# Scattered rows of a fused long convolution and mixture of experts: smaller staging units, another spread of the row DMAs, fewer cleared pages, no flush

## The chip, the cores and the metric

The kernel runs on one core of a Trainium2 chip. The time is device microseconds of one execution, first to last instruction and what the runtime lays around it; the median of several runs counts. Five engines work beside each other, each through its own list of instructions, strictly in order: TensorE (PE, matrix products; PEld is its weight load), VectorE (DVE), ScalarE (ACT), GpSimd (POOL) and SyncE (SP, which only starts DMAs). An instruction that waits holds everything behind it in its own list, and nothing else.

## What is computed

Cut to its core, the reference is a causal convolution over 10048 positions by way of Fourier transforms, for 4 batch entries of 128 channels, gated by its input, and then a mixture of experts: each of the 40192 rows goes to one of 16 experts, a two-layer network 128 to 1024 to 128.

```python
y = irfft(rfft(x * v, 2 * S) * rfft(h_filt, 2 * S)[None], 2 * S)[:, :S]
x = (x * y).reshape(4 * 10048, 128)
for g in range(4):                 # group by argmax of x @ w_group
    for e in range(4):             # expert by argmax of x @ w_expert[g]
        h = np.maximum(x[mine] @ w1[g, e], 0.0)
        out[mine] = g_w * e_w * (h @ w2[g, e])
```

## The kernel before

**Stages.** Batch entries are called batches 0 to 3 here. After the filter's own transform the function `conv` runs a loop over b. Each pass has two stages. The first is the forward transform of batch b (43 parts of three channels, `dft_blocks`) together with the inverse transform of batch b - 1 (22 steps j, `turned` and `inverse_blocks`, which ends in the product with x, L692). The second, 40 steps of two frequencies each, multiplies by the filter's spectrum: `middle` (two products on DVE, L605 and L608, then a sum and a difference on POOL, L606 and L609, which write a tile y) and, four steps later, `back` (the matmul that reads y, L617). The last pass, b = 4, has only the inverse transform of batch 3. In the trace these stages are called here forward/inverse 1, 2, 3 (inverse of batches 0, 1, 2), middle 0, 1, 2, 3, the last inverse, the last choice of experts, and the experts.

**Routing.** When a batch's rows are there, `chosen` writes them to HBM (`xyd`) and computes expert and weight of each row; `ranked` then counts rows per expert and computes for each row its address `adr` in a paged buffer `prow` in HBM. A page holds 256 rows of one expert. Both are generators, of which one step at a time is taken between the steps of the stages; so the routing of batch b runs in the middle stage b + 1 and at the head of the next stage.

**Rows into pages.** A batch's rows stand in 79 blocks of 128. Each block is one indirect DMA, started by POOL (`put`, L343), which writes its 128 rows to the addresses in `adr`. The rows come from HBM through a staging tile `stg`: `stage` starts the load on SP (L335) and adds the row's number and weight by a small copy on POOL (L336). Load and copy write a buffer that earlier puts read, and so wait until these have landed. Before the puts of a batch come eight indirect DMAs that empty the open ends of its last pages (`clear`, L357). All of these stand in a list `self.scatters`; each call of `scatter(n)` issues up to n of them, so the calls' arguments in `conv` spread them over the stages. Pages that hold no row of the first assignment are emptied once, by plain DMAs from POOL in middle 1 (`clear_rest`, L326).

**POOL's other work.** In the forward/inverse stages 2 and 3 POOL also computes a difference for each part (`eo`, L437) that the forward transform needs; in the last inverse every other product L692; among the experts, the low half of one weight matrix per page (`wl`, L1224) and the indirect DMAs that write the output (L1280).

**Experts.** `work` runs 164 pages, one after the other, in a software pipeline. `fetch` issues the scatters that are left, early enough for the pages that need them. `rest` handles pages beyond the 164 if there are any.

**Buffers of the last inverse.** `xo` (the gate's input, loaded on SP, L660) and `yt` (L689, L690) take turns in one ring of four buffers.

A scheduler may move instructions that no fixed order holds; most of those named here are held in program order on their engine.

Of the kernel before, what the change touches and what calls it, by code (L numbers as in the profile page):

```python
# [12 lines left out]
F32 = mybir.dt.float32  # L13
# [30 lines left out]
RW = 130  # L44
ZR = 4
LAGS = 3
STG = 2
EVERY = 2
LATER = 48
CHOSEN = -(-NB // 4) + 2  # L50
# [83 lines left out]
class Kernel:  # L134
# [59 lines left out]
    def conv(self, ctx, right):  # L194
        tc, nc, d = self.tc, self.nc, self.d
        cp = ctx.enter_context(tc.tile_pool(name="cconst", bufs=1))
        zp = ctx.enter_context(tc.tile_pool(name="z", bufs=1))
        self.psA = ctx.enter_context(tc.tile_pool(name="psA", bufs=3, space=PSUM, reuse_waits="tile"))
        self.psT = ctx.enter_context(tc.tile_pool(name="psT", bufs=3, space=PSUM, reuse_waits="tile"))
        self.psO = ctx.enter_context(tc.tile_pool(name="psO", bufs=2, space=PSUM, reuse_waits="tile"))  # L200
        self.psr = lambda shape, name: self.psO.tile(shape, F32, tag="po", name=name)
        self.fa = cp.tile([NR, 2, 2 * NB], F32, name="fa")

        self.z = zp.tile([128, KM + 16, 2, 128], F32, name="z")
        nc.vector.memset(self.z[:, NB:], 0.0)
        ahead = ExitStack()
        made, folded = [], []
        with ExitStack() as c2:
            self.filter(c2, ahead, made, folded)
        bp = ctx.enter_context(tc.tile_pool(name="back", bufs=1))  # L210
        self.fi = bp.tile([128, 2, 5, NB], F32, name="fi")
        nc.sync.dma_start(self.fi.rearrange("p h a t -> p (h a t)"), d["c_fi"])


        inner = ExitStack()
        xyp = inner.enter_context(tc.tile_pool(name="xy", bufs=1, reuse_waits="tile"))
        self.sp = inner.enter_context(tc.tile_pool(name="stream", bufs=2, reuse_waits="tile"))
        routing, self.scatters = iter(()), []

        self.anchor, self.loose = None, []  # L220
        for b in range(self.nbat + 1):
            last = b == self.nbat
            if last:
                ahead.close()
                inner.close()
                self.sp = ctx.enter_context(tc.tile_pool(name="stream", bufs=2, reuse_waits="tile"))
                weights = self.first_weights(right)
                xy = self.z.rearrange("p k s d -> p (k s) d")[:, :NB]
            elif b > 0:
                xy = xyp.tile([128, NB, D], F32, tag="xy", name=f"xy{b - 1}")  # L230
            parts = groups(D, GD) if not last else []
            if b == 1:
                self.router_consts()
            self.run_ahead(b, 0, made, folded)
            for j, (d0, n) in enumerate(groups(120, GI) + [(120, 4), (124, 4)]):
                if b > 0 and j % 2 == 0:
                    tts = self.turned(d0, min(2 * GI, D - d0))
                for i in range(2 * j, min(2 * j + 2, len(parts))):
                    self.run_ahead(b, i, made, folded)
                    self.scatter(1 + (i % 4 == 0))  # L240
                    self.dft_blocks(*folded[i])
                    if b > 0 and i % 2 == 0:
                        self.inverse_blocks(b - 1, xy, d0, n, tts)
                if last:
                    self.inverse_blocks(b - 1, xy, d0, n, tts)
                    next(weights, None)
                    if j == 1:
                        for p in self.all[:XG]:
                            p.load()
                for _ in range(3 if last else 1):  # L250
                    next(routing, None)
                if last:
                    self.scatter(1 + j % 2)
            made, folded = [], []
            if b > 0:
                oh = self.rp.tile([128, NE, NB], F32, tag="oh", name="oh")
                en = self.entries.tile([128, NB, 2], F32, tag="en", name="en")
                routing = chain(self.chosen(b - 1, xy, oh, en), self.ranked(b - 1, oh, en))
                if last:
                    for _ in range(CHOSEN):  # L260
                        next(routing)
            if not last:
                back = []
                for i, (k0, n) in enumerate(groups(NB, 2)):
                    back.append(self.middle(b, k0, n))
                    if len(back) > LAG:
                        self.back(*back.pop(0))
                    if b == 1 and i % 4 == 1:
                        self.clear_rest(i // 4)
                    self.scatter(NB if b == self.nbat - 1 and i == 37 else i < 37)  # L270
                    if i % 4 != 3 if i < 30 else i % 2:
                        next(routing, None)
                for args in back:
                    self.back(*args)
        return routing
# [44 lines left out]
    def clear_rest(self, i):  # L320

        q0 = self.nbat * SEQ // TP
        qs = range(q0, self.pages.n)[i::10]
        for q in qs:
            dst = self.d["prow"][q * TP : q * TP + TP].rearrange("(p z) c -> p z c", z=ZR)
            self.tc.keep_in_program_order(self.nc.gpsimd.dma_start(dst, self.empty[: TP // ZR]))  # L326

    def stage(self, k):

        while self.staged <= min(k, len(self.units) - 1):  # L330
            u = self.units[self.staged]
            n = u.n
            u.rows = self.entries.tile([128, 4, RW], F32, tag="stg", name="stg", bufs=STG)
            src = self.d["xyd"][u.b * 128 * NB : (u.b + 1) * 128 * NB].rearrange("(p t) c -> p t c", p=128)
            self.nc.sync.dma_start(u.rows[:, :n, 0:128], src[:, u.t0 : u.t0 + n])  # L335
            self.beyond(self.nc.gpsimd.tensor_copy(u.rows[:, :n, 128:130], u.en[:, u.t0 : u.t0 + n]))  # L336
            self.staged += 1

    def put(self, u, t):

        self.stage(u.k + STG - 1)
        n = self.pages.n * TP
        ins = self.nc.gpsimd.indirect_dma_start(  # L343
            self.d["prow"],
# [308 lines left out]
    def inverse_blocks(self, b, xy, d0, n, tts):  # L653
# [30 lines left out]
                )  # L684
        oo = sp.tile([64, GI, NB], F32, tag="oo", name="oo")
        nc.scalar.copy(oo[:, :n], po[64:128, :n])
        pool, tag, bufs = (self.ap, "y", NY) if b < self.nbat - 1 else (sp, "spec", NSPEC)
        yt = pool.tile([128, GI, NB], F32, tag=tag, name="yt", bufs=bufs)
        nc.vector.tensor_tensor(yt[0:64, :n], po[0:64, :n], oo[:, :n], ALU.add)  # L689
        nc.vector.tensor_tensor(yt[64:128, :n], po[0:64, :n], oo[:, :n], ALU.subtract)  # L690
# [108 lines left out]
    def ranked(self, b, oh, en):  # L799
# [122 lines left out]
        v.memset(pos[64:128, NB - 1 : NB], BIGID)  # L922
        adr = self.entries.tile([128, NB], I32, tag="adr", name="adr")
        v.tensor_copy(adr, pos)
        for t0, n in groups(NB, 4):
            u = Unit(b, len(self.units), t0, n, adr, en)
            self.units.append(u)
            self.scatters += [(b, lambda u=u, t=t: self.put(u, t), self.tick + LAGS, u) for t in range(t0, t0 + n)]
# [96 lines left out]
    def rest(self, count, q):  # L1025

        with self.tc.If(count > q):
            self.work(self.all[q : q + 4])
            if q + 4 < self.pages.n:
                self.rest(count, q + 4)  # L1030

# [351 lines left out]
```

## Time and profile before

| what | us |
|---|---|
| median of three runs | 2227.9 |
| lowest and highest of them | 2226.0, 2235.4 |
| the profiled execution, whole | 2243.6 |
| its span, first to last instruction | 2241.8 |
| PE busy in it (89%) | 2006.3 |
| DVE busy (77%) | 1719.4 |
| POOL busy (63%) | 1402.3 |
| ACT busy (61%) | 1364.4 |

The profile is of one execution. Shares over the whole span mix stages with different limits: the experts (from about 1166 us on) are a dense stretch of matmuls, while in the stages of the convolution different engines set the pace. So the tables of the prediction are by stage. In a row of groups stand the line, engine, operation, tiles (written from read), shape and count, then busy time and mean duration in ns of one, then the idle time of the engine just before them with what ended it. In a row of waits stand who waited for whom, the total in us, how often, and the longest. In a row of stretches stand each engine's busy time with its number of instructions, the clock that PE was granted, the share of the DMA engines and GB/s. Timeline rows begin with start and duration in us.

### The profile page before, as it was taken

The page shows a single profiled execution, that of the slowest core. Times are in us where ns is not written, and L with a number is a line of the kernel's source. Part 1 is how long each engine was busy: PE and PEld are TensorE (multiplying, and loading weights), DVE is VectorE, ACT ScalarE, POOL GpSimd, SP SyncE. Part 2 cuts the span into 40 slices and gives each one's busy share as a digit, 9 for nine tenths or more (in the row PEclk, how much of TensorE's full clock was granted, in tenths as well). Part 3 has the DMA queues.
Part 4 walks back from the last instruction along what each step waited for, and adds up shares of the span by engine and source line. Part 5 has one row for each costly group of instructions (what it writes and reads, how often), then busy time and mean ns, then how long its engine had stood idle before and what let it go on. Part 6 is the DMA issues. An engine that isn't in the chain of part 4 may idle for free. (4 is left out here: it accounts for less than half of the span.)

```text
span 2241.8 us, 54150 instructions
## 1 busy us (share of the span) xinstructions
PE 2006.3 (89%) x18062; PEld 1824.2 (81%) x18062; DVE 1719.4 (77%) x3647; ACT 1364.4 (61%) x3005; POOL 1402.3 (63%) x1521
## 2 busy tenths in 40 slices
PE   8989999987888788885879999999999999999997
PEld 8867787766766577664659999999999999999996
DVE  5687776896567776668459989899899778888885
ACT  6642454433443244332458888888878778888885
POOL 2167402886778866785525667688878785555554
PEclk9999999988899788998989999999999999999998
DMA  4798756965677655774654444546555554444442
GB/s 126 250 247 283 223 149 199 360 195 165 172 243 265 190 142 169 243 267 149 206 176 136 128 143 143 149 145 184 151 151 159 153 146 133 129 128 125 125 125 61
DMA packets 260641, 394.26 MB, mean 176 GB/s; under 512 B 33319, under 2 KB 133266, under 8 KB 260352
## 3 DMA queue, kind: packets, MB, share of 16 engines
q1 hardware_dynamic: 225024, 318.01, 46.9%
q0 software_dynamic: 25824, 57.16, 7.3%
q10 hardware_dynamic: 9504, 15.54, 2.7%
q8 instruction: 146, 2.39, 0.5%
q14 instruction: 143, 1.17, 0.2%
HBM read 303.24 MB, written 88.37 MB: 175 GB/s over the span
## 5 line engine op out<-in xcount | busy, mean ns | idle before, releaser
L1244 DVE SCALAR_TENSOR_TENSOR hl<-ph,hh 128x512 fp32r<-128x512 f32 x656 | 445.9, 685 | 117.2 <-ACT hh L1243 91.8
L1243 ACT ACTIVATE hh<-ph 128x512 fp32r<-128x512 f32 x656 | 393.3, 605 | 130.5 <-PE ph L1237 68.7
L1280 POOL DMA_INDIRECT out<-os,to x328 | 347.4, 1059 | 93.7 <-issue 80.8
L1254 PE MATMUL py<-hh,wh 128*128 128x256 f32 x1312 | 398.7, 304 | 0.0
L343 POOL DMA_INDIRECT prow<-stg,adr x316 | 344.7, 1091 | 82.1 <-issue 47.7
L1256 PE MATMUL py<-hh,wl 128*128 128x256 f32 x1312 | 373.9, 285 | 12.8 <-POOL wl L1224 12.3
L1235 PE MATMUL ph<-xh,wh 128*128 128x256 f32 x1312 | 373.3, 284 | 4.3 <-ACT wh L1217 2.5
L1237 PE MATMUL ph<-xh,wl 128*128 128x256 f32 x1312 | 373.1, 284 | 0.6 <-DVE wl L1224 0.6
L1236 PE MATMUL ph<-xl,wh 128*128 128x256 f32 x1312 | 372.6, 284 | 0.0
L1255 PE MATMUL py<-hl,wh 128*128 128x256 f32 x1312 | 371.6, 283 | 0.0
L1224 POOL TENSOR_TENSOR wl<-ws,wh 128x512 fp32r<-128x512 f32 x162 | 219.5, 1355 | 220.5 <-ACT wh L1217 216.9
L1256 PEld LDWEIGHTS py<-hh,wl 128*128 128x128 f32 x1312 | 251.6, 192 | 16.3 <-POOL wl L1224 16.3
L1235 PEld LDWEIGHTS ph<-xh,wh 128*128 128x128 f32 x1312 | 252.9, 193 | 5.0 <-ACT wh L1217 2.7
L1237 PEld LDWEIGHTS ph<-xh,wl 128*128 128x128 f32 x1312 | 253.0, 193 | 1.2 <-DVE wl L1224 1.2
L1236 PEld LDWEIGHTS ph<-xl,wh 128*128 128x128 f32 x1312 | 253.0, 193 | 0.1
L624 ACT COPY z<-pbp 128x512 f32<-128x512 f32 (+1 forms) x160 | 92.6, 581 | 263.3 <-PE pbp L617 225.9
L1255 PEld LDWEIGHTS py<-hl,wh 128*128 128x128 f32 x1312 | 252.8, 193 | 0.0
L1254 PEld LDWEIGHTS py<-hh,wh 128*128 128x128 f32 x1312 | 252.0, 192 | 0.0
L1224 DVE TENSOR_TENSOR wl<-mw,wh 128x512 fp32r<-128x512 f32 x328 | 233.5, 712 | 0.0
L447 PE MATMUL psb<-z,bt 128*128 128x256 f32 x790 | 203.6, 389 | 33.1 <-DMA bt<-c_b 15.4
L606 POOL TENSOR_TENSOR y<-t 128x256 f32<-128x256 f32 (+1 forms) x160 | 119.3, 746 | 167.1 <-DVE t L605 161.4
L1217 ACT CAST wh<-ws 128x512 fp32r<-128x512 f32 x328 | 206.6, 630 | 10.1 <-PE ph L1237 8.4
(232 smaller groups left out, 4488.7 us busy)
## 6 DMA issues: line engine op xcount, KB each, us to landing
ws<-m_w SPq DMA_DIRECT2D x328, 256.0 KB
ht<-hspec SPq DMA_DIRECT2D x156, 256.0 KB
xv<-xv_in SPq DMA_DIRECT2D x131, 288.0 KB
bt<-c_b SPq DMA_DIRECT2D x95, 256.0 KB
xg<-prow SPq DMA_DIRECT2D x164, 130.0 KB
bp<-c_bp SPq DMA_DIRECT2D x76, 256.0 KB
stg<-xyd SPq DMA_DIRECT2D x76, 256.0 KB
xyd<-xy SPq DMA_DIRECT2D x57, 256.0 KB
```

Source lines behind the costliest of these rows:

```text
L343: ins = self.nc.gpsimd.indirect_dma_start(self.d["prow"], bass.IndirectOffsetOnAxis(ap=u.adr[:, t : t + 1], axis=0), u.rows[:, t - u.t0], ...
L1217: k.fix(k.nc.scalar.copy(hi, self.matrix(i, half, self.ea)))
L1224: ins = v.tensor_tensor(lo, self.matrix(i, half, self.ed), self.wh[i][half].bitcast(F32), ALU.subtract)
L1235: k.fix(nc.tensor.matmul(ph[:, j], wh, self.xh, start=True, stop=False))
L1236: k.fix(nc.tensor.matmul(ph[:, j], wh, self.xl, start=False, stop=False))
L1237: k.fix(nc.tensor.matmul(ph[:, j], wl, self.xh, start=False, stop=True))
L1243: k.fix(nc.scalar.activation(hh, ph, AF.Relu))
L1244: k.fix(nc.vector.scalar_tensor_tensor(hl, ph, 0.0, hh.bitcast(F32), ALU.max, ALU.subtract))
L1254: k.fix(nc.tensor.matmul(self.py, wh, self.hh[c], start=(c == 0), stop=False))
L1255: k.fix(nc.tensor.matmul(self.py, wh, self.hl[c], start=False, stop=False))
L1256: k.fix(nc.tensor.matmul(self.py, wl, self.hh[c], start=False, stop=(c == NC - 1)))
L1280: ins = k.nc.gpsimd.indirect_dma_start(k.d["out"], bass.IndirectOffsetOnAxis(ap=self.to[:, h : h + 1], axis=0), o[:, h], None, bounds_chec ...
```

## The change

Six things change. A staging unit has two blocks instead of four, and there are four buffers instead of two, which is the same memory. The refill is started at the first put of a unit for the unit two ahead, into the buffer of the unit two back, instead of one ahead into the buffer of the unit just finished. The row DMAs are spread in another way: in the forward/inverse stage one per part, and from part 12 on two at every odd part (before: one, and two at every fourth); in the middle stage three in four steps (before: one at each of the first 37 steps). At step 37 of the last middle stage nothing is flushed any more; what is left goes out in the last inverse, and the first page loads move from its step 1 to its step 8, behind the puts of batches 0 and 1. `clear_rest` empties 7 pages instead of 47, and pages beyond 164 are each guarded by an own condition. In the last inverse `yt` has a ring of two buffers of its own, and `xo` keeps the ring of four.

```diff
-STG = 2
+UB, STG = 2, 4
@@ conv, forward/inverse stage
-                    self.scatter(1 + (i % 4 == 0))
+                    self.scatter(1 + (i >= 12 and i % 2))
...
-                    if j == 1:
+                    if j == 8:
+                        self.scatter(sum(1 for s in self.scatters if s[0] < self.nbat - 2))
                         for p in self.all[:XG]:
                             p.load()
@@ conv, middle stage
-                    self.scatter(NB if b == self.nbat - 1 and i == 37 else i < 37)
+                    self.scatter(i % 4 != 3)
@@ clear_rest
-        qs = range(q0, self.pages.n)[i::10]
+        qs = range(q0, self.pages.usual)[i::10]
@@ stage
-            u.rows = self.entries.tile([128, 4, RW], F32, tag="stg", name="stg", bufs=STG)
+            u.rows = self.entries.tile([128, UB, RW], F32, tag="stg", name="stg", bufs=STG)
@@ put
-        self.stage(u.k + STG - 1)
+
+        self.stage(u.k + STG // 2)
@@ inverse_blocks
-        pool, tag, bufs = (self.ap, "y", NY) if b < self.nbat - 1 else (sp, "spec", NSPEC)
+        pool, tag, bufs = (self.ap, "y", NY) if b < self.nbat - 1 else (sp, "yt", 2)
@@ ranked
-        for t0, n in groups(NB, 4):
+        for t0, n in groups(NB, UB):
@@ rest
-            self.work(self.all[q : q + 4])
+            self.work(self.all[q : q + 1])
+            for p in self.all[q + 1 : q + 4]:
+                with self.tc.If(count > p.q):
+                    self.work([p])
```

The lines of the kernel after stand two lower from `put` on (L345 is the put, L337 the copy, L439 the difference, L608 and L611 the sums, L694 the last product, L359 the clears).

**Forward/inverse 2, list of POOL, a stretch of its second half.** L437 is the difference of a part; the number behind `stg` names the buffer's filling. Before:

```order
L437 TENSOR_TENSOR eo_6834<-xv_6778 96x3x64
L336 COPY stg_6837<-en_4438 128x4x2
L343 DMA prow<-stg_6680,adr_6068 52224x130 x2
L437 TENSOR_TENSOR eo_6882<-xv_6831 96x3x64
L343 DMA prow<-stg_6680,adr_6068 52224x130
L437 TENSOR_TENSOR eo_6899<-xv_6879 96x3x64
L343 DMA prow<-stg_6680,adr_6068 52224x130
L437 TENSOR_TENSOR eo_6941<-xv_6896 96x3x64
L336 COPY stg_6944<-en_4438 128x4x2
```

The same stretch of the list after the change:

```order
L439 TENSOR_TENSOR eo_7227<-xv_7201 96x3x64
L345 DMA prow<-stg_7103,adr_6028 52224x130
L439 TENSOR_TENSOR eo_7269<-xv_7224 96x3x64
L337 COPY stg_7272<-en_4438 128x2x2
L345 DMA prow<-stg_7162,adr_6028 52224x130 x2
L439 TENSOR_TENSOR eo_7328<-xv_7266 96x3x64
L337 COPY stg_7331<-en_4438 128x2x2
L345 DMA prow<-stg_7210,adr_6028 52224x130
L439 TENSOR_TENSOR eo_7373<-xv_7325 96x3x64
L345 DMA prow<-stg_7210,adr_6028 52224x130
L337 COPY stg_7379<-en_4438 128x2x2
```

Before, the copy into a new filling (6944) stands right behind the last put of the unit whose buffer it takes over, and four puts come between copies. After, a copy (7331) takes over a buffer whose puts stand a whole unit further back (the two puts of 7162 lie between), a copy comes after every two puts, and there are three puts to two differences.

**End of middle 3 and head of the last inverse, list of POOL.** L606 and L609 make the y tiles of the last steps, L357 the clears, L692 products of the last inverse. Before:

```order
L609 TENSOR_TENSOR y_12105<-t1_12109 128x2x128
L343 DMA prow<-stg_11996,adr_9413 52224x130 x3
L606 TENSOR_TENSOR y_12160<-t0_12161 128x2x128
L606 TENSOR_TENSOR y_12175<-t0_12176 128x128
L609 TENSOR_TENSOR y_12175<-t1_12179 128x128
L357 DMA prow<-empty_81,fidx_11955 13056x520 x8
L609 TENSOR_TENSOR y_12160<-t1_12164 128x2x128
L692 TENSOR_TENSOR z_103<-yt_12325,xo_12304 128x6x79
```

After:

```order
L345 DMA prow<-stg_12048,adr_9433 52224x130
L608 TENSOR_TENSOR y_12222<-t0_12223 128x128
L611 TENSOR_TENSOR y_12222<-t1_12226 128x128
L345 DMA prow<-stg_12123,adr_9433 52224x130
L694 TENSOR_TENSOR z_103<-yt_12375,xo_12354 128x6x79
L337 COPY stg_12430<-en_10819 128x2x2
L345 DMA prow<-stg_12123,adr_9433 52224x130
L337 COPY stg_12436<-en_10819 128x2x2
L345 DMA prow<-stg_12187,adr_9433 52224x130
L359 DMA prow<-empty_81,fidx_12026 13056x520
L694 TENSOR_TENSOR z_103<-yt_12528,xo_12507 128x6x79
L359 DMA prow<-empty_81,fidx_12026 13056x520 x3
```

Eight clears stood ahead of the last difference that makes a y; now they stand between the products of the last inverse, and the y tiles have one put at a time between them.

**Last inverse, list of SP.** L660 (L662 after) loads `xo`, L997 (L999) the experts' weights, L335 (L336) fills a staging buffer. Before:

```order
L335 DMA stg_12874<-xyd 128x4x128
L660 DMA xo_12919<-x_out 128x474
L997 DMA mw1_12217<-m_w1 128x2x512
L660 DMA xo_12948<-x_out 128x474
L997 DMA mw1_12217<-m_w1 128x2x512
L335 DMA stg_12977<-xyd 128x4x128
L660 DMA xo_13019<-x_out 128x474
```

After:

```order
L336 DMA stg_12904<-xyd 128x2x128
L662 DMA xo_12910<-x_out 128x474
L999 DMA mw1_12264<-m_w1 128x2x512
L336 DMA stg_12939<-xyd 128x2x128
L662 DMA xo_12981<-x_out 128x474
L999 DMA mw1_12264<-m_w1 128x2x512
L662 DMA xo_13010<-x_out 128x474
L999 DMA mw1_12264<-m_w1 128x2x512
L336 DMA stg_13036<-xyd 128x2x128
```

Before, a refill stands ahead of every second load of `xo`; after, refills of half the size stand ahead of two in three, and each waits for puts issued a unit earlier.

## The prediction

> **What bounds the kernel now.** I read the stretches by stage first, since shares of the whole span mix stages with different limits.
>
> ```profile
> core 0: us, PE busy (x) PEld busy (x) DVE busy (x) ACT busy (x) POOL busy (x), PEclk, DMA share, GB/s
> 252.00:372.00 120.00, 109.46 (x1556) 96.34 (x1558) 90.88 (x185) 60.39 (x108) 2.06 (x4) 0.94 0.55 151
> 372.00:471.00 99.00, 91.16 (x585) 71.23 (x581) 83.09 (x198) 38.80 (x93) 78.55 (x121) 0.98 0.95 322
> 471.00:628.00 157.00, 125.70 (x1594) 106.49 (x1594) 110.30 (x194) 62.45 (x111) 111.86 (x132) 0.86 0.58 168
> 628.00:747.00 119.00, 96.08 (x563) 72.68 (x563) 82.79 (x193) 39.10 (x93) 95.42 (x123) 0.95 0.79 257
> 747.00:903.00 156.00, 127.78 (x1594) 107.93 (x1594) 110.79 (x222) 61.34 (x111) 104.90 (x124) 0.84 0.56 160
> 903.00:1045.00 142.00, 102.26 (x581) 75.96 (x577) 101.04 (x271) 40.51 (x95) 111.41 (x139) 0.89 0.66 228
> 1045.00:1131.00 86.00, 73.07 (x1061) 61.11 (x1062) 45.50 (x68) 37.45 (x65) 36.61 (x39) 0.96 0.58 190
> 1166.00:1450.00 284.00, 275.85 (x2258) 273.87 (x2259) 254.42 (x593) 234.90 (x529) 181.44 (x162) 0.98 0.47 140
> 1450.00:1870.00 420.00, 400.31 (x3296) 394.55 (x3295) 363.67 (x698) 339.83 (x761) 338.55 (x319) 1.00 0.52 155
> 1870.00:2242.00 372.00, 355.55 (x2985) 354.91 (x2983) 287.06 (x622) 306.41 (x686) 207.18 (x177) 0.98 0.39 117
> ```
>
> The rows are forward/inverse 1, middle 1, forward/inverse 2, middle 2, forward/inverse 3, middle 3, the last inverse, and three stretches of the experts. The stages without puts are much shorter: forward/inverse 120 us against 157 and 156, middle 99 against 119 and 142. PE is busy 91 of 99 us in middle 1 but only 126 of 157 in forward/inverse 2. Among the experts PE is busy over 95%, so little can be gained there. Next the waits, first over the whole span and then of the last inverse, to see what puts have to do with it.
>
> ```profile
> POOL stg L336 <- DMA prow<-stg,adr: 70.7, 39, 3.8
> SPq L335 <- DMA prow<-stg,adr: 290.3, 78, 9.2
> ...
> SPq L335 <- DMA prow<-stg,adr: 31.6, 7, 9.2
> DVE z L692 <- DMA xo<-x_out: 18.3, 7, 4.3
> PE po L670 <- DVE yt L690: 9.9, 4, 4.1
> ```
>
> POOL stands 70.7 us in the small copy, until the last put of the buffer's old unit has landed, and SP 290 us in the refill, with everything queued behind it. Whether that counts is told by POOL's groups in stretches where puts run: forward/inverse 2 (530 to 620 us), forward/inverse 3 (815 to 895) and middle 2 (640 to 730).
>
> ```profile
> L343 POOL DMA_INDIRECT prow<-stg,adr x35 | 38.6, 1102 | 9.1 <-issue 5.1 <-POOL stg L336 3.2 <-DVE yt L690 0.6
> L437 POOL TENSOR_TENSOR eo<-xv 96x192 f32<-96x192 f32 x26 | 21.1, 812 | 0.5
> L336 POOL COPY stg<-en 128x8 f32<-128x8 f32 x8 | 2.8, 349 | 19.0 <-DMA prow<-stg,adr 19.0
> ...
> L343 POOL DMA_INDIRECT prow<-stg,adr x30 | 34.7, 1156 | 8.4 <-issue 4.0 <-POOL stg L336 2.3 <-DVE xv L423 1.5
> L437 POOL TENSOR_TENSOR eo<-xv 96x192 f32<-96x192 f32 x23 | 14.9, 650 | 0.4
> L336 POOL COPY stg<-en 128x8 f32<-128x8 f32 x8 | 2.1, 266 | 20.1 <-DMA prow<-stg,adr 15.7 <-issue 4.4
> ...
> L343 POOL DMA_INDIRECT prow<-stg,adr x29 | 29.1, 1003 | 8.4 <-issue 4.6 <-POOL stg L336 3.8
> L609 POOL TENSOR_TENSOR y<-t 128x256 f32<-128x256 f32 x29 | 22.6, 780 | 0.0
> L606 POOL TENSOR_TENSOR y<-t 128x256 f32<-128x256 f32 x29 | 21.9, 755 | 2.7 <-DVE t L605 2.2
> L336 POOL COPY stg<-en 128x8 f32<-128x8 f32 x6 | 1.4, 237 | 6.0 <-DMA prow<-stg,adr 6.0
> ```
>
> In the first stretch the busy times and the idle times add up to 91 of 90 us: **POOL never waits for anybody but its own puts**. So POOL sets the pace there, and PE gets its differences (L437) or sums (L606, L609) only as fast as POOL comes to them. The stall of 19 us in 90 is on the path; so is every put, and every copy.
>
> **The change part by part.** Durations are of this execution, 2243.6 us long (span 2241.8); the three plain runs have a median of 2227.9, 15.7 less, so I take the difference from the profile off the median.
>
> *Forward/inverse 2.* A put costs (38.6 + 9.1 - 3.2) / 35 = 1.27 us with its gap, a difference 0.81, a copy with the gap behind it (2.8 + 3.2) / 8 = 0.75. Before, 26 parts took 90 us, 6.92 per two parts. After, from part 12 on, two parts carry three puts, two differences and 1.5 copies without stall: 3.81 + 1.62 + 1.13 = 6.56. Over 15.5 pairs that is 5.6 us less: **-6**. The stall goes, but most of it is paid back in more puts (54 puts and clears in the stage against 49) and in twice the copies. The new refill could stall too; two puts and two differences, about 4 us, now lie between the old unit's last put and the copy, and the longest stall so far was 3.8. I take it as gone.
>
> *Forward/inverse 3.* The same sum from its own rows: put 1.36, difference 0.65, copy 0.55; 80 us for 23 parts, 6.96 per pair; after 4.08 + 1.30 + 0.83 = 6.21. Over 15.5 pairs **-12**. Both stages cannot go below the pace of forward/inverse 1, 120 us for 21.5 pairs, 5.58.
>
> *Middle 2 and 3.* 29 steps took 90 us, 3.10 each. After, a step has both sums (22.6 + 21.9 + 2.7) / 29 = 1.63, 0.75 puts of 1.16, and 0.375 copies of 0.9: 0.87 + 0.33 + 1.63 = 2.83. Over 38 steps -10; SP no longer holds the loads of the spectrum behind a refill, for which I add 2: **-12 each**. The floor is middle 1, 99 us for 40 steps, 2.48.
>
> *The flush.* POOL's list and PE at the end of middle 3, and that stretch:
>
> ```profile
> 1029.58 0.45 POOL L609 TENSOR_TENSOR y<-t 128x128 f32<-128x128 f32 x1
> 1030.20 1.05 POOL L357 DMA_INDIRECT prow<-empty,fidx  x1 [0.17 <-issue]
> ...
> 1040.14 1.12 POOL L357 DMA_INDIRECT prow<-empty,fidx  x1 [0.30 <-issue]
> 1041.28 0.74 POOL L609 TENSOR_TENSOR y<-t 128x256 f32<-128x256 f32 x1
> 1042.08 1.22 PE L617 MATMUL pbp<-y,bp 128*128 128x256 f32 x2 [15.17 <-POOL y L609]
> ...
> 1029.00:1042.00 13.00, 0.00 (x0) 0.00 (x0) 12.93 (x50) 0.00 (x0) 10.69 (x12) 0.50 0.52 191
> ```
>
> Eight clears hold one sum back by 11 us, and PE stands 15.2. But DVE was busy 12.93 of those 13 us, with `ranked`. That work does not vanish: it now falls beside the products of the last inverse, on the same DVE, which is busy 45.5 of 86 us there and has room, though not at its head. Between 0 and 15, I take half: **-8**. The eight clears go to POOL's list in the last inverse, which then issues four puts fewer, 25 against 29, and POOL is busy only 37 of 86 us there.
>
> *The last inverse.* DVE waits 18.3 us for `xo`, whose load stands behind a refill on SP (31.6 us in seven waits) and behind a ring that it shares with `yt`. Both go. What reached PE is nearer to its own 9.9 us of waiting for `yt`: between 0 and 18, **-7**.
>
> *Clearing.*
>
> ```profile
> L326 POOL DMA_DIRECT2D prow<-empty x47 | 25.0, 538 | 0.0
> ```
>
> Forty issues of 0.54 us leave POOL in middle 1 and 5.2 MB leave a stage whose DMA share is 0.95. But PE was busy 91 of its 99 us, so between 0 and 8: **-2**.
>
> *The experts.*
>
> ```profile
> PE py L1256 <- POOL wl L1224: 12.3, 13, 2.5
> ```
>
> Here POOL gets more: 67 refills against 31, 36 copies of 0.75, and seven puts of batch 2 that were done earlier before; 27 + 9 us, less a few us of stall. In the first two stretches POOL is busy 181 of 284 and 339 of 420 us, so most of it hides in 184 free us; if that cover were gone it would cost 36, and at best the 12.3 us vanish. I take **+3**. The conditions for pages beyond 164 are not entered either way: 0, as in the row of the last stretch, which has only the pages' matmuls.
>
> Sum: -6 - 12 - 12 - 12 - 8 - 7 - 2 + 3 = **-56**. 2243.6 becomes 2188 for such an execution, and the median 2227.9 becomes **2172**.
>
> **Rivals.** *Half of it.* POOL's time is read from rows in which it shares the stage with a busy DVE; with the stalls gone DVE runs denser, puts and copies stretch, and other waits (DVE for its input, PE for ACT) take over part of it. For it speaks that puts took 1.10 and 1.16 us in the forward/inverse stages against 1.00 in middle 2. Half of 56 gives 2200.
>
> *The floor.* Once POOL is out of the way, stages fall to the pace of those without puts: 15.5 x (6.92 - 5.58 and 6.96 - 5.58) = 42 and 38 x 2 x (3.10 - 2.48) = 47, with flush, inverse and clearing at 15, 10 and 2: -116, 2112. Against it: three puts, two differences and the copies cannot be issued in 5.58 us by the rows above.
>
> *Another wait in its place.* The puts land no earlier than before, and a refill of half the size starts a transfer twice as often; if the refill itself arrives late, the stall only moves from the copy to the put. Then the spread and the extra puts eat the rest: about 2222. Against it: a filling is asked for four puts, some 8 us, ahead of its use, as before.
>
> *Slower: the copies.* Each of the 80 added copies stands in the list of the engine that sets the pace.
>
> ```profile
> L336 POOL COPY stg<-en x80: 182/193/1052, 509.8 to 1835.8; 128x8 f32<-128x8 f32 x76, 128x6 f32<-128x6 f32 x4
> ```
>
> The longest took 1.05 us. At that price, 0.70 above mine, the 93 copies that the stages of the convolution have after the change (against 49) add 65 us, and a quarter of the 67 among the experts 12: +21 in all, 2249. It decides from a copy of 0.75 + 56 / 93 = 1.35 us on. Against it stands the median of 193 ns. The Trainium skill, "SBUF — State Buffer", section "Who interferes with whom", speaks for it: a GpSimd instruction that reads SBUF is kept out for the whole length of a VectorE instruction with two SBUF inputs, and such instructions are what DVE runs in the forward/inverse stages. The row of before agrees in that copies there mean 349 and 266 ns against 237 in middle 2, but shows a full instruction's wait only in its maximum.
>
> **How the numbers follow.** About 0.5%, 11 us, is what a measurement of this kernel can tell from no change. The forecast, 2172, gets 0.60: POOL's sums close on their windows, and the removed stall and flush are read directly. Half gets 0.17, the floor 0.10, another wait 0.08, slower copies 0.05. Faster by over 0.5% are the first three, 0.87; within 0.5% 0.08; slower 0.05. The forecast's own bounds (flush 0 to 15, last inverse 0 to 18, clearing 0 to 8, experts -12 to +36) reach some 35 us to either side; half's 2200 lies inside, the floor is taken in only in part: 2132 to 2212.
>
> **What would show it.** Right: POOL's wait for landed puts falls from 70.7 us to below 10 and SP's 290 to a fraction; forward/inverse 2 and 3 last about 151 and 144 us, middle 2 about 107; middle 3 has no gap of PE near 15 us, and middle 3 with the last inverse together take some 200 instead of 228; DVE no longer waits for `xo`; the experts last as long as before within a few us. Wrong: copies near 1 us, a wait of puts for the refill in place of the old one, a last inverse that grows by what middle 3 lost because `ranked` holds up `yt`, or experts in which PE's 12.3 us of waiting for `wl` have doubled.

## The result, and the profile after

Before: median 2228.0 us of 4 runs (2226.0 to 2235.4). After: **2166.8** (2165.1 to 2174.2). The ratio is 0.9726, 95% interval 0.9694 to 0.9758, so the change saves 61 us. The forecast was 2172, with a range of 2132 to 2212. The profiled execution after the change took 2168.2 us, close to its median, while the one of before (2243.6) lay 15.6 above its own. So a second execution of before was profiled (span 2220.7), and the stages below are held against that one.

The stretches of the changed kernel, from one stage's first matmul to the next's, in the columns of the prediction's first table: middle 1, forward/inverse 2, middle 2, forward/inverse 3, middle 3, last inverse, experts.

```profile
core 0: us, PE busy (x) PEld busy (x) DVE busy (x) ACT busy (x) POOL busy (x), PEclk, DMA share, GB/s
370.60:461.60 91.00, 86.51 (x564) 69.30 (x560) 77.50 (x199) 38.00 (x91) 60.36 (x85) 1.00 0.91 298
461.60:606.60 145.00, 122.23 (x1595) 104.84 (x1595) 110.41 (x191) 62.80 (x112) 121.75 (x149) 0.88 0.62 178
606.60:723.40 116.80, 97.42 (x577) 74.72 (x575) 82.25 (x194) 39.96 (x95) 90.42 (x124) 0.95 0.84 263
723.40:872.20 148.80, 122.16 (x1582) 103.99 (x1582) 110.22 (x222) 61.18 (x109) 120.36 (x141) 0.85 0.59 169
872.20:991.10 118.90, 100.36 (x581) 76.94 (x577) 87.45 (x212) 41.19 (x96) 92.97 (x129) 0.93 0.74 242
991.10:1080.50 89.40, 71.66 (x1069) 60.45 (x1069) 66.04 (x132) 38.99 (x65) 49.75 (x54) 0.96 0.67 217
1103.50:2166.40 1062.90, 1028.35 (x8537) 1021.84 (x8537) 917.99 (x1917) 874.45 (x1973) 755.16 (x696) 0.99 0.47 140
```

Middle 1 takes 91.0 us, with PE at full clock (1.00); forward/inverse 2 and 3 are still 25 to 29 us longer than forward/inverse 1 (120.2). Middle 2, forecast at 107, stands at 116.8. The waits over the whole span, which answer to the rows of POOL's copy, SP's refill and the loads of `xo` before:

```profile
SPq L336 <- DMA prow<-stg,adr: 426.1, 141, 11.6
...
DVE z L694 <- DMA xo<-x_out: 15.9, 4, 4.7
...
PE py L1261 <- POOL wl L1229: 11.7, 18, 1.3
...
POOL z L694 <- DMA xo<-x_out: 4.1, 1, 4.1
...
POOL stg L337 <- DMA prow<-stg,adr: 2.1, 5, 0.8
```

POOL's wait for landed puts went from 70.7 to 2.1 us, as forecast. SP's wait in the refill did not fall to a fraction of 290: **it rose to 426**. Per wait it is a little shorter (426.1 / 141 = 3.0 against 290.3 / 78 = 3.7 us), but there are nearly twice as many (the second profile of before has 327.1 us in 92 waits). DVE still waits 15.9 us for `xo`, which was to vanish.

### The profile page after: what moved, and what is told of

Its sections match the earlier page's. It is cut to its first block, busy times and chain, and to the rows that moved or that the text cites. A ratio compares the mean times of both kernels' runs of the same rounds, so it can differ in the third digit from the quotient of the medians.

```text
span 2166.4 us, 54337 instructions
## 1 busy us (share of the span) xinstructions
PE 1986.7 (92%) x18062; PEld 1816.9 (84%) x18062; DVE 1728.6 (80%) x3647; ACT 1360.1 (63%) x3005; POOL 1421.5 (66%) x1561
## 4 chain that ended last, share of the span: by engine, by line
PE 59%; DVE 11%; DMA 7%; POOL 7%; issue 4%; ACT 1%; SPq 0%; ACTq 0%; POOLq 0%; DVEq 0%
PE py L1261 7%; PE py L1259 7%; PE py L1260 7%; PE ph L1242 7%; PE ph L1240 7%; PE ph L1241 7%; PE psb L449 3%; PE pbp L619 3%; DMA ht<-hspec 2%; PE psa L378 2%; DMA xv<-xv_in 2%; POOL prow L345 2%; PE ptm L1273 2%; PE px L1197 2%; POOL out L1285 1%
## 5 line engine op out<-in xcount | busy, mean ns | idle before, releaser
L1285 POOL DMA_INDIRECT out<-os,to x328 | 357.2, 1089 | 92.8 <-issue 74.6
L345 POOL DMA_INDIRECT prow<-stg,adr x316 | 345.7, 1094 | 70.4 <-issue 35.3
L1261 PE MATMUL py<-hh,wl 128*128 128x256 f32 x1312 | 373.8, 285 | 11.7 <-POOL wl L1229 11.7
L1261 PEld LDWEIGHTS py<-hh,wl 128*128 128x128 f32 x1312 | 251.1, 191 | 15.9 <-POOL wl L1229 15.6
L608 POOL TENSOR_TENSOR y<-t 128x256 f32<-128x256 f32 (+1 forms) x160 | 117.2, 732 | 202.8 <-DVE t L607 195.6
L1229 DVE TENSOR_TENSOR wl<-mw,wh 128x512 fp32r<-128x512 f32 x328 | 245.3, 748 | 0.0
L449 PE MATMUL psb<-z,bt 128*128 128x256 f32 x790 | 203.9, 389 | 34.5 <-DMA bt<-c_b 15.1
L1222 ACT CAST wh<-mw 128x512 fp32r x328 | 206.7, 631 | 0.0
```

The lines of the kernel that those rows point to most:

```text
L345: ins = self.nc.gpsimd.indirect_dma_start(self.d["prow"], bass.IndirectOffsetOnAxis(ap=u.adr[:, t : t + 1], axis=0), u.rows[:, t - u.t0], ...
L449: nc.tensor.matmul(ps[:, i], bt[:, i], self.z[:, k0 + i], start=True, stop=True,)
L1229: ins = v.tensor_tensor(lo, self.matrix(i, half, self.ed), self.wh[i][half].bitcast(F32), ALU.subtract)
L1261: k.fix(nc.tensor.matmul(self.py, wl, self.hh[c], start=False, stop=(c == NC - 1)))
L1285: ins = k.nc.gpsimd.indirect_dma_start(k.d["out"], bass.IndirectOffsetOnAxis(ap=self.to[:, h : h + 1], axis=0), o[:, h], None, bounds_chec ...
```

## The experiments

Two theories stood after this result. *The sum holds*: POOL's stall and the flush were the price, and each part is worth what its term says. *SP has taken over*: a refill that waits on SP holds the loads of the spectrum (`ht`, `bt`) and of `xo`, so the middles lost their gain to a new wait. Stage durations in us, each from PE's first matmul of a stage to that of the next, read off the timeline of each run's profile; the median is that of the run's timed executions. Each row is one execution: the two profiles of before differ by up to 4.0 us in a stage and by 10.0 among the experts, so a single difference below that is weak evidence by itself.

| kernel | fwd/inv 2 | middle 2 | fwd/inv 3 | middle 3 | last inv. | experts | span | median |
|---|---|---|---|---|---|---|---|---|
| before, second profile | 153.6 | 119.3 | 153.3 | 140.0 | 97.4 | 1068.1 | 2220.7 | 2222.5 (one) |
| units alone | 151.0 | 118.0 | 151.2 | 135.9 | 80.9 | 1057.9 | 2186.3 | 2189.6 |
| spread alone | 160.7 | 121.5 | 153.8 | 139.4 | 95.5 | 1070.0 | 2229.7 | 2234.4 |
| no flush alone | 154.4 | 119.3 | 155.7 | 124.1 | 95.9 | 1077.4 | 2214.0 | 2218.4 |
| ring alone | 153.2 | 123.3 | 153.0 | 139.7 | 96.9 | 1068.8 | 2224.5 | 2225.0 |
| clears alone | 154.2 | 120.9 | 153.3 | 144.0 | 94.5 | 1067.6 | 2217.9 | 2219.4 |
| after | 145.0 | 116.8 | 148.8 | 118.9 | 89.3 | 1062.9 | 2166.4 | 2166.8 |
| after, large units | 161.9 | 116.9 | 157.3 | 123.0 | 96.5 | 1071.7 | 2210.1 | 2211.9 |
| after, old spread | 151.0 | 114.7 | 148.5 | 117.1 | 84.8 | 1063.4 | 2165.1 | 2174.5 |
| after, with flush | 144.5 | 114.6 | 148.8 | 137.4 | 82.3 | 1056.3 | 2168.9 | 2171.8 |
| after, one ahead | 148.2 | 105.3 | 147.9 | 107.9 | 80.3 | 1059.9 | 2133.4 | **2138.9** |
| after, refill on POOL | 154.7 | 111.4 | 151.3 | 120.6 | 86.8 | 1089.8 | 2198.7 | 2204.5 |
| one ahead, two in inverse | 145.2 | 104.4 | 150.8 | 107.9 | 93.4 | 1053.6 | 2138.3 | 2140.9 |

Middle 1 lasts 91.0 in every kernel without the 40 clears and 95.7 to 97.8 in the others.

**The kernel before once more** (no edit).

> The kernel before once more, for a second profiled execution. The experts of the first one lasted 1078.1 us, those of the changed kernel 1062.9, though nothing in the change should shorten them. If the 15 us are that one execution (it was 2243.6 against a median of 2227.9), this profile's experts last 1060 to 1066 and its other stages stay within 1 to 2 us: 120.9, 98.0, 157.2, 118.7, 155.8, 142.4, 93.4 for forward/inverse 1, middle 1, forward/inverse 2, middle 2, forward/inverse 3, middle 3, last inverse. If the change does shorten the experts, they last 1075 to 1081 again, and a whole execution is near 2243.

The experts lasted 1068.1 us: 10 of the 15 us were that one execution, 5 are left for the change. In the three kernels below with the same puts among the experts and large units (spread, ring and clears alone) they last 1067.6 to 1070.0, so it is the first execution that stands apart; PE waited 13.7 us there for ACT's copy `ys`, against 5.3 in the second. The other stages moved by 4 us at most, more than the 1 to 2 expected.

**Units alone** (the lines that take the size from `UB`, in `stage` and `ranked`, are left out here).

```diff
-STG = 2
+UB, STG = 2, 4
-        self.stage(u.k + STG - 1)
+        self.stage(u.k + STG // 2)
```

> The kernel before with the staging units alone: two blocks, four buffers, two units ahead. If POOL's stall is on the path and sets the pace of the forward/inverse stages, removing 19 us of 90 and 20 us of 80 there and paying one more copy per four puts (0.75 us each) leaves -13 in each of the two stretches, some -18 in each whole stage, about 0 in the middles (6 us of stall against 7 us of copies): -35 to -45 in all, near 2188, and this part is most of the gain. If the change gains by its other spread of the puts and the units only make it possible, this gives -10 or less (2218 or more). SP: if its wait in the refill grows because a refill now waits for puts that were issued shortly before, its waits are above 380 us here too, against 290 before.

Ratio 0.9840 (0.9807 to 0.9873): the total fits the first theory, the places do not. Forward/inverse 2 and 3 gave 2.6 and 2.1 us, not 18 each; the last inverse gave 16.5 and the experts 10.2. POOL's waits in forward/inverse 2, before (second profile) and with small units:

```profile
POOL stg L336 <- DMA prow<-stg,adr: 18.6, 9, 3.9
...
POOL eo L437 <- PE psa L376: 3.0, 2, 2.2
```

```profile
POOL eo L437 <- PE psa L376: 18.8, 10, 3.0
```

The stall of 18.6 us left, and a wait of 18.8 us for PE took its place: with the old spread POOL was the pace only as long as it stalled. Where the gain was instead, the last inverse shows. Its stretch before (second profile):

```profile
1032.20:1129.50 97.30, 76.97 (x1068) 64.10 (x1069) 46.79 (x72) 38.37 (x65) 44.26 (x46) 0.89 0.55 177
```

and with small units:

```profile
1023.90:1104.80 80.90, 69.88 (x1068) 59.40 (x1068) 46.63 (x72) 38.31 (x65) 46.97 (x56) 0.99 0.66 214
```

The waits in these two stretches, before first:

```profile
DVE z L692 <- DMA xo<-x_out: 25.9, 8, 5.5
...
POOL z L692 <- DMA xo<-x_out: 18.8, 6, 4.9
...
PE po L670 <- DVE yt L690: 12.7, 5, 4.1
```

```profile
DVE z L692 <- DMA xo<-x_out: 21.7, 8, 4.5
...
POOL z L692 <- DMA xo<-x_out: 7.3, 5, 2.6
...
PE po L670 <- DVE yt L690: 4.9, 4, 1.6
```

PE waits 7.8 us less for `yt`, and its 1068 matmuls take 7.1 us less at a granted clock of 0.99 instead of 0.89. SP's wait was 419 us here, above the 380 named: the longer wait comes with the units.

**Spread alone** (both `scatter` arguments of the change, the flush kept).

> The kernel before with the other spread of the puts alone, the flush and the large units kept. Each middle has 0.25 puts of 1.16 us less per step, -11 in middle 2 and in middle 3; each forward/inverse stage has about five puts more, each with its share of stall some 1.8 us, +9. Additive parts: -4 in all, same (2224). If the middles are paced by POOL, middle 2 shortens to 108; if another engine or SP's held loads pace it, it stays above 114, and the whole is slower, 2235.

Ratio 1.0047 (1.0029 to 1.0065). Middle 2 did not get shorter (121.5): it still held 35 puts, as before, because forward/inverse 2 passed only the same 44 in its 160.7 us and left the added six over, ahead of the middle's first sum in POOL's list. With the stall in that list more puts to a part only pile up.

**No flush alone.**

```diff
-                    if j == 1:
+                    if j == 8:
+                        self.scatter(sum(1 for s in self.scatters if s[0] < self.nbat - 2))
-                    self.scatter(NB if b == self.nbat - 1 and i == 37 else i < 37)
+                    self.scatter(i < 37)
```

> The kernel before without the flush at step 37 of the last middle stage, and with the first page loads at step 8. The prediction's term says -8 (0 to -15): PE's gap of 15.2 us goes, and the routing's work on DVE falls beside the last inverse, which grows by some 7. If PE's gap was the whole price, middle 3 with the last inverse shortens by 15. If DVE's work is what had to be done anyway, they shorten by 0 to 2.

Middle 3 and the last inverse lost 17.4 us together: PE's gap was the whole price there, and `ranked` on DVE did not hold the inverse up. But the kernel gained only 5 (ratio 0.9978, 0.9960 to 0.9996): the experts were 9.3 longer, with 133 puts among them instead of 127, and PE's wait for `wl` there went from 13.0 to 19.4.

**Ring alone** (`yt` in two buffers of its own).

> The kernel before with the own ring for yt alone. The prediction put -7 on the last inverse for this and for the smaller refills together, and the units alone already shortened that stage from 97.4 to 80.9 us. If the shared ring is what makes SP late with xo, the ring alone gives -5 or more there (below 92). If it is the refill that SP stands in, the ring alone gives 0 to -2, DVE's and POOL's waits for xo stay at some 40 us together, and the whole is the same (2222 to 2227).

Ratio 1.0001 (0.9982 to 1.0021), last inverse 96.9 against 97.4: the shared ring had no price that shows.

**Clears alone** (7 pages instead of 47, own conditions beyond page 164).

> The kernel before with 7 cleared pages instead of 47 and an own condition for each page beyond 164. The prediction said -2 in middle 1 (0 to -8). In the changed kernel middle 1 lasts 91.0 us against 97.1 and 98.0. If the missing clears are the whole reason, middle 1 lasts 90 to 92 here and every other stage as before: -6 to -7, near 2218. If the conditions beyond 164 cost time at the end, the whole gains less than middle 1 does.

Ratio 0.9968 (0.9951 to 0.9985), 7 us, and middle 1 went from 97.1 to 91.0. The conditions cost nothing. The end of the program even got shorter: from PE's last matmul to the end of the span 14.2 us in the second profile of before and 11.7 here, and no more than 11.9 in any kernel that has this edit. What fills the time behind the last output there the profiles do not show.

**The change with the old spread.**

```diff
-                    self.scatter(1 + (i >= 12 and i % 2))
+                    self.scatter(1 + (i % 4 == 0))
-                    self.scatter(i % 4 != 3)
+                    self.scatter(i < 37)
```

> The changed kernel with the old spread: one put per part and two at every fourth, one at each of the first 37 steps of a middle. Alone, on the kernel before, the new spread cost time (ratio 1.0047, some +10 us; forward/inverse 2 grew by 7 us). If the parts add up, taking it out of the changed kernel gains 10 us: 2157. If the spread needs the small units (without a stall behind every unit the doubled puts no longer pile up), taking it out costs: forward/inverse 2 back to 151, as with the units alone, forward/inverse 3 to 151, the middles 1 to 3 longer: 2174 to 2180.

The ratio to before is 0.9784 (0.9753 to 0.9816), against 0.9726 for the whole change; the intervals just overlap, and its four runs lie between 2166.9 and 2179.0. Forward/inverse 2 went back to 151.0 as the second theory of the expectation says, but the middles and the last inverse got shorter, by 1.8 to 4.5 us; the profiled execution (2166.9) is also the lowest of the four. With small units the new spread is worth between nothing and 8 us; alone it cost 10.

**The change with large units.**

```diff
-UB, STG = 2, 4
+UB, STG = 4, 2
-        self.stage(u.k + STG // 2)
+        self.stage(u.k + STG - 1)
```

> The changed kernel with four blocks to a unit, two buffers, refilled one unit ahead, as before; spread, ring, clears and the missing flush stay. If the units alone are worth what they gave on the kernel before (ratio 0.984, 35 us), this is 2202. If spread and units lean on each other, the other parts without the units are worth no more than -10 to -15 together: 2210 to 2215, with POOL's stall in the copy back at 65 to 75 us and PE's wait for wl among the experts above that of the changed kernel (11.7 us).

Ratio 0.9947 (0.9930 to 0.9964): without the units the rest is worth 12 us, with them the change is worth 61. Units alone gave 35, so they and the rest lean on each other by some 14 us, above all in forward/inverse 2 (units alone 151.0, the rest alone 161.9, both 145.0): three puts to two parts are paid only where no stall of 77.9 us stands in POOL's list.

**The refill one unit ahead.**

```diff
-        self.stage(u.k + STG // 2)
+        self.stage(u.k + 1)
```

> The changed kernel with one edit: the refill started at the first put of a unit is for the next unit, into the buffer of three units back, instead of two ahead into the buffer of two units back. Middle 2 lasts 116.8 us in the changed kernel, where 107 was predicted; SP waits 426 us in the refill and DVE 26.7 for the spectrum, PE 15.1 for its table. Theory, SP holds the middles: the wait of the refill for the unit before last holds the loads behind it; with a buffer whose puts lie a unit further back SP's wait falls below 150 us, the two waits of 42 us together fall below 20, and middle 2 and 3 shorten by 6 to 10 us each: 2147 to 2155. Rival, the middles are paced by DVE and POOL: SP's wait falls as much, the middles stay within 2 us of 116.8 and 118.9, the whole is 2160 to 2170. Second rival, the refill comes too late: puts wait for the load of their own rows, 1 us or more at each of some 40 units, and the whole is 2180 to 2210.

**2138.9 us, ratio 0.9619 (0.9596 to 0.9642), faster than both kernels.** The middles fell to 105.3 and 107.9, the last inverse to 80.3. The waits of middle 2: before (second profile), after, and one ahead.

```profile
SPq L335 <- DMA prow<-stg,adr: 52.3, 13, 6.1
...
DVE t L605 <- DMA ht<-hspec: 8.4, 5, 4.1
POOL stg L336 <- DMA prow<-stg,adr: 8.4, 6, 2.5
...
PE psb L447 <- DMA bt<-c_b: 7.0, 4, 3.2
...
POOL y L606 <- DVE t L605: 6.2, 3, 2.8
```

```profile
SPq L336 <- DMA prow<-stg,adr: 52.4, 16, 6.8
...
DVE t L607 <- DMA ht<-hspec: 16.6, 7, 5.1
POOL y L608 <- DVE t L607: 16.4, 15, 2.6
...
PE psb L449 <- DMA bt<-c_b: 5.7, 3, 4.8
```

```profile
SPq L336 <- DMA prow<-stg,adr: 32.7, 12, 6.1
...
DVE t L607 <- DMA ht<-hspec: 9.0, 4, 3.9
POOL y L608 <- DVE t L607: 8.5, 4, 3.0
...
PE psb L449 <- DMA bt<-c_b: 0.5, 1, 0.5
```

Read down the chain: SP stands in the refill, the spectrum comes late, DVE waits for it, POOL waits for DVE. In the change POOL's 8.4 us of stall had turned into 16.4 us of waiting for DVE. One unit ahead, the refill takes over the buffer of three units back, whose puts lie two further back in POOL's list. SP's wait over the whole span fell only to 376, not below 150, since it stayed as it was in the forward/inverse stages and among the experts (179 us), where it holds nothing that is late; in the two middles and the last inverse it fell by 60 of 152 us. Puts waited 0.9 us in all for their own rows. The waits for the spectrum and for PE's table `bt` fell from 41.8 us together to 28.5, not below 20: in middle 2 both fell, but in middle 3, which gained 11 us as well, the table's fell from 7.5 to 0.3 and the spectrum's rose from 8.9 to 13.2. There PE idled 4.9 us less and its matmuls took 5.7 less, at a granted clock of 0.98 instead of 0.93. That SP's refill wait holds the middles is so shown by the edit; through which of the held loads, only for middle 2.

**The refill issued by POOL.**

```diff
-            self.nc.sync.dma_start(u.rows[:, :n, 0:128], src[:, u.t0 : u.t0 + n])
+            self.beyond(self.nc.gpsimd.dma_start(u.rows[:, :n, 0:128], src[:, u.t0 : u.t0 + n]))
```

> The changed kernel with the refill issued by POOL instead of SP. SP then waits for no put at all, so whatever the middles lose to SP's queue is given back; in exchange POOL issues one more DMA per unit, some 0.55 us each (the clears in middle 1 took 0.54), 15 in a middle and 25 in a forward/inverse stage. Theory, SP holds the middles: DVE's wait for the spectrum and PE's for its table fall from 42 us together to below 20, and middle 2 and 3 lose no more than POOL's 8 us give back: 110 to 117. Rival, the middles are paced by DVE and POOL: the waits fall, and the middles grow by POOL's 8 us, 123 to 127. Under both the forward/inverse stages 2 and 3, where POOL is busy 122 of 145 us, grow by 5 to 14 us each: 2175 to 2200 in all.

The stretch of middle 2, and POOL's group of refills in it:

```profile
615.70:727.10 111.40, 97.10 (x578) 73.39 (x576) 87.48 (x192) 39.73 (x94) 104.22 (x142) 0.97 0.84 274
```

```profile
L336 POOL DMA_DIRECT2D stg<-xyd x14 | 10.6, 755 | 1.1 <-DMA prow<-stg,adr 1.1
```

In middle 2 no wait for `ht` was left, and the stage shortened by 5.4 us although POOL had 10.6 us of refills more: a second sign that SP held it. Middle 3 grew by 1.7, to 120.6, outside the 110 to 117 expected; POOL was busy 111.6 us of it, and PE waited 13.3 for POOL's `y`. Forward/inverse 2 and the experts paid (9.7 and 26.9 us), the latter with 34.6 us of PE's wait for `wl`. The whole took 2204.5 (ratio 0.9919, 0.9892 to 0.9947), above the 2175 to 2200 expected.

**The change with the flush back.**

> The changed kernel with the flush at step 37 of the last middle stage back, and the first page loads at step 1 of the last inverse again. On the kernel before, taking the flush out shortened middle 3 by 15.9 and the last inverse by 1.5 us, and lengthened the experts by 9.3, where PE's wait for wl rose from 13.0 to 19.4 us: 5 to 7 us in all. If the price among the experts comes from the seven puts of batch 2 that move there, the experts here are 5 to 9 us shorter than 1062.9 and the wait for wl below 9 us, and the two stages 17 longer: 2173 to 2180. If those 9 us were only a difference between two executions, the experts stay within 2 us of 1062.9 and the whole is 2180 to 2186.

2171.8, ratio 0.9761 (0.9737 to 0.9785), 5 us over the change, though the intervals overlap. Middle 3 grew by 18.5, the last inverse shrank by 7.0 and the experts by 6.6, with 127 puts among them instead of 133 (so six move, not seven) and the wait for `wl` at 6.5 instead of 11.7. That is the second pair of kernels in which the missing flush goes with longer experts, so a price there is likely, by single executions.

**One ahead, and two scatters at every step of the last inverse** (`scatter(1 + j % 2)` becomes `scatter(2)`).

> The changed kernel with the refill one unit ahead, as in the run that gave 2138.9, and with two scatters at every step of the last inverse instead of one and two by turns, so that some eleven puts of batch 2 leave the experts. POOL was busy 50 of 89 us in the last inverse. If puts among the experts cost PE about 0.5 us each through wl, and POOL's idle time in the last inverse hides them there, the experts shorten by 4 to 6 us and the last inverse grows by less than 3: 2133 to 2138. If POOL's products in the last inverse are held up by them, that stage grows by 8 us or more and the whole is 2140 to 2146.

Among the experts 123 puts were left of 133. They shortened by 6.3 us, the wait for `wl` fell from 11.1 to 5.8, and the last inverse grew by 13.1, as the second expectation has it: 2140.9, no gain.

## Why the prediction was right in the sum, and where not

Against the second profile of before, the terms came out so (us):

| term | predicted | measured |
|---|---|---|
| forward/inverse 2 | -6 | -8.6 |
| forward/inverse 3 | -12 | -4.5 |
| middle 2 | -12 | -2.5 |
| middle 3 with the flush | -20 | -21.1 |
| last inverse | -7 | -8.1 |
| clearing (middle 1) | -2 | -6.1 |
| experts | +3 | -5.2 |

The terms add up to -56.1 where -56 was forecast, and the medians to -61. Four of the seven are off by 4 us or more, in both directions, so that the sum came out is in part luck.

- **POOL's stall and its pace.** Right that the stall goes, and right in forward/inverse 2 for units and spread together, which is how the pairs were counted. "The stall of 19 us in 90 is on the path; so is every put, and every copy" was too much: units alone took the stall out and moved that stage by 2.6 us. (The stage held 52 puts and clears before and 58 after, not 49 and 54, which does not enter the sum.)
- **Forward/inverse 3: the count of pairs was wrong.** From 795 to 867 us the changed kernel did 24 parts in 72 us, 6.0 to a pair, even under the 6.21 forecast. (Before, the second profile did 22 in its own 72 us from 814.9 on, 6.5 to a pair and not the 6.96 of the first.) But the first few of the 15.5 pairs had no three puts. POOL's puts in 756 to 796 us, parts 12 to 20:

```profile
L345 POOL DMA_INDIRECT prow<-stg,adr x6 | 6.3, 1045 | 5.2 <-issue 3.1 <-DVE r L969 1.9 <-POOL stg L337 0.3
L439 POOL TENSOR_TENSOR eo<-xv 96x192 f32<-96x192 f32 x9 | 6.2, 692 | 2.6 <-issue 2.6
```

Six puts and nine differences in 40 us: the first put of the stage stands in POOL's list only behind part 16, since `ranked` is still at work on the addresses. Which engine set the pace there no row shows alone (DVE busy 30.9 us, PE 29.1, POOL 25.5). By PE, the first 20 parts took 86.0 us before (second profile) and 86.3 after, the 22 behind them 65.5 and 60.8: the gain lies wholly in the second half. The ranking also stands at the head of forward/inverse 2, whose first four parts in the second profile of before are this stretch:

```profile
466.00:494.60 28.60, 22.38 (x204) 17.25 (x204) 28.49 (x62) 9.54 (x18) 22.48 (x29) 0.80 0.47 137
```

DVE is busy 28.5 of 28.6 us. The first put comes 42.4 us into the stage, so no spread of puts shortens that: the first eight of the 43 parts took 48 us before and 47 after, against 26 in forward/inverse 1. So 21 of the 25 us by which the stage still exceeds forward/inverse 1 lie in its head.

- **Middle 2: the failed step.** It was "SP no longer holds the loads of the spectrum behind a refill". SP's wait in middle 2 stayed at 52 us, more of it fell on `ht`, and the rival "another wait in its place" held in this stage, with SP in the place that it gave to the puts. POOL's sum for the step fits: with SP's wait at 33 us the stage took 105.3 against the 107 forecast.
- **Middle 3, the flush and the last inverse** came out near the forecast by luck: three errors cancel. Middle 3 itself gave 2.6 instead of 12 (137.4 with the flush back), for middle 2's reason. The flush gave 18.5 there, not 8, and took back 7.0 in the last inverse and 6.6 among the experts, net 5 (by single executions: the last inverse took 80.3, 84.8 and 89.3 us in three kernels with small units and no flush). The last inverse alone gave 15.1 (82.3 with the flush back), twice its term, and the units alone gave 16.5; "and behind a ring that it shares with `yt`" was wrong, the ring gave 0.5. "Both go" was wrong for the refill too: SP's wait there was 42.3 us, as before (44.9).
- **Clearing** was mis-sized: 6.1 and not 2, though inside its bounds of 0 to 8.
- **Experts: the sign was wrong.** Of the 5.2 us, 2.4 are the shorter end of the program, which came with the conditions that were entered at 0; PE's wait for `wl` fell by 1.3, and its matmuls took 1.7 less. Over the kernels the experts go with that wait, but for the first profile of before, in which PE waited for `ys`:

| kernel | PE's wait for `wl` | experts |
|---|---|---|
| one ahead, two in inverse | 5.8 | 1053.6 |
| units alone | 6.4 | 1057.9 |
| after, with flush | 6.5 | 1056.3 |
| after, one ahead | 11.1 | 1059.9 |
| after, old spread | 11.5 | 1063.4 |
| after | 11.7 | 1062.9 |
| before, first profile | 12.3 | 1078.1 |
| ring alone | 12.6 | 1068.8 |
| before, second profile | 13.0 | 1068.1 |
| spread alone | 14.1 | 1070.0 |
| clears alone | 14.4 | 1067.6 |
| after, large units | 18.0 | 1071.7 |
| no flush alone | 19.4 | 1077.4 |
| refill on POOL | 34.6 | 1089.8 |

The units take 9 to 10 us off (1068.1 to 1057.9, 1071.7 to 1062.9); the six puts that the missing flush pushes there add 7 to 9.

- **Rivals.** "The copies" fell: they stay far from the deciding 1.35 us. All copies of the changed kernel have (shortest, median, longest in ns)

```profile
L337 POOL COPY stg<-en x160: 176/213/1777, 496.5 to 1776.4; 128x4 f32<-128x4 f32 x156, 128x2 f32<-128x2 f32 x4
```

The group of 507 to 600 us, in forward/inverse 2:

```profile
L337 POOL COPY stg<-en 128x4 f32<-128x4 f32 x22 | 9.6, 438 | 0.2 <-DMA prow<-stg,adr 0.2
```

Ahead of the experts 19 copies took more than 400 ns, and 16 of these end within 0.1 us of the end of a product of two SBUF tiles on DVE (L425 or L694); the one of 1777 ns began during one such product and ended with the next. That fits the rule of the Trainium skill that the prediction named ("SBUF — State Buffer", section "Who interferes with whom"), as the price of 17 of the 51 copies of forward/inverse 2 and 3 and of none of the 13 in middle 2, not as that of each copy. "The floor" (2112) was not reached by the change; one ahead came within 27 us of it.

Left open: what the spread is worth beside the small units (0 to 8 us), by which of the loads behind SP middle 3 was held, and how much of the last inverse's gain is PE's clock and how much the wait, since both moved together.

## What to carry to other kernels

A wait on a queue that only starts DMAs costs what stands behind it: ask of each stall which loads follow in the same list, stage by stage, since the same wait is free among the experts (where engines wait under 2 us for the loads behind it) and holds a middle for 11 us. A buffer scheme is judged by how far back the last reader of the buffer lies, not by how early the refill is asked for. And price a term by the rows of the very steps it covers: a pace read in the second half of a stage does not hold in its head, and a removed stall is worth only the distance to the next wait.

## What was not expected of the hardware

In the last inverse the same 1068 matmuls kept PE busy 77.0 us at a granted clock of 0.89 and 69.9 at 0.99, the latter where PE waited less: 7.1 of that stage's 16.5 us are shorter matmuls. Other runs of this stage follow the clock in the same way: 74.0 us at 0.90, 72.6 at 0.94, 71.7 at 0.96, 70.3 at 1.00. A refill started by POOL occupied it for a median of 773 ns (382 on SP in the changed kernel), while the plain clears that it also starts took a median of 535 ns.
